# The last two chunks' second product in seven parts instead of eight, with SyncE in a planned order

## The chip, the core and the metric

The kernel runs on one core of a Trainium2 chip. Engines work side by side and meet through semaphores: TensorE (PE) multiplies, with its weight loads on a second row (PEld); VectorE (DVE), ScalarE (ACT) and GpSimd (POOL) do everything elementwise; SyncE (SP) issues nearly all DMAs. The metric is device microseconds (us) of one launch.

## The reference, cut to what matters

Inputs: q, k, v of shape 8 x 8 x 576 x 64 (batch, heads, tokens, width), g_norm of 64, and two weight matrices in 64-bit floats, w_in (512 x 2048) and w_out (2048 x 512).

```
kv  = einsum('bhsd,bhse->bhde', k, v)
x   = einsum('bhsd,bhde->bhse', q, kv)
x   = x / sqrt(mean(x*x, -1) + 1e-6) * g_norm        # to 4608 x 512
h   = x @ w_in                                       # first product, 4608 x 2048
g   = h * cos(h)
out = g @ w_out                                      # second product, 4608 x 512
```

## The kernel before

**Precision.** TensorE multiplies in a reduced 32-bit form (F32R), so each large factor is split into a high and a low half, and a product takes three matmuls: high by high, high by low, low by high. All large matmuls are 128 x 128 by 128 x 512.

**Tiling.** The 4608 tokens are nine chunks of 512. The width of 2048 is 16 strips of 128, called j, or eight pairs of strips, called m. The first three chunks (`PLAIN = 3`) are multiplied directly. Their 48 steps (`steps`, L285) each make one strip of h (`stage1_part`, L1007: 12 matmuls), then g of it (`act_part`, L1041: ACT and DVE), then add its share to four output banks (`stage2_part`, L1075: 12 matmuls). The order of steps is chunk 0 strips 0 to 3, chunk 1 strips 0 to 7, chunk 0 strips 4 to 15, chunk 1 strips 8 to 15, chunk 2. When a chunk is left unfinished its four banks are copied out and stored (`out_part`, L1108, the tensor `part`).

The other six chunks are three pairs. Their first product is Strassen's in the Winograd form: 2 x 2 blocks, seven products A11, S1, S2, A12, S4, S3, A22 instead of eight. `cross_part` (L1301) makes the seven operands from x (four of them sums), `sums_part` (L1208) the four sums of w_in for each m; the other three operands are strips as they are. `quad_part` (L1375) multiplies them for one (pair, m), 42 matmuls, adds the products together, and makes four tiles of g. The second product of these chunks is direct: a unit (`units`, L1168) is one strip j of one chunk. `split_part` (L1473) makes the high and low half of g, ACT casting and DVE or POOL subtracting, and `gather_part` (L1488) multiplies four token tiles by three matmuls: g is stationary (`lhsT`), w_out moves (`rhs`), 12 matmuls a unit, 16 units a chunk.

**Weights.** Each strip is loaded as 64-bit words (`w_loads`, L563), rebuilt and split (`w_part`, L948), and stays in SBUF for the first three chunks. Beside that, split strips are stored back to DRAM: `keep_in` (L1190, to `wq`), `keep_out` (L1201, to `wod`), and the sums to `wq` (L1239). When chunk 2 has used a strip, `freed_in` and `freed_out` (L1246, L1257) give its SBUF to the Strassen stage: the places of w_out strips 8 to 11 take weights of the first product (`t_win`), 12 to 15 those of the second (`t_wout`), strips 0 to 7 hold g and x. `load_in` and `load_out` (L1275, L1289) then stream the weights back, 512 KB a DMA.

**What sets the order.** While the program is built, `Order` (L50) plays every part as a process against guessed durations. At each point it takes the operation that can start first, ties going to the due time (`due`, L303, plus a table of offsets, `haste`, L310). Buffers are `Tokens` (taken and given back), and parts wait for `Event`s. `gates[i]` fires when step i begins on PE: `KEEP, SUMS = 16, 18` (L299) say from which step on the stores and sums may start. PE, ACT, DVE and POOL are then held to this order:

```
    pe, act, dve, pool = (Pinned(x) for x in (nc.tensor, nc.scalar, nc.vector, nc.gpsimd))
```

SyncE is not in that line. Its DMAs are issued as `nc.sync.dma_start`, and where they fall in SyncE's queue is decided by the tile framework's own scheduler. `Order` itself counts a load of several DMAs as one SyncE operation and one DMA time (`load`, L464).

**The end.** The last output tile (L1111 to L1124) is copied in two halves, one by ACT and one by DVE, each stored by its own engine's queue, in rows of 1 KB.

Of the kernel before, what the change touches and what calls it, by code (L numbers as in the profile page):

```python
# [48 lines left out]

class Order:  # L50
# [8 lines left out]
    LAT = 0.14  # L59
# [10 lines left out]
    def spawn(self, gen, t=0.0):  # L70
        proc = Proc(gen, t)
        self.live.add(proc)
        self.advance(proc, None)

    def advance(self, proc, value):
        while True:
# [18 lines left out]
            else:  # L95
# [5 lines left out]
                proc.t = max(proc.t, t)  # L101

# [32 lines left out]
    def run(self):  # L135
        while self.pending:
            best = None
            for item in self.pending:
                prio, seq, t, options, _ = item
                if len(options) == 1:  # L140
                    e, d = options[0][:2]
                else:
                    ends = [
                        max(t, self.busy.get(o[0].rstrip("*"), 0.0) + self.ahead(o[0].rstrip("*"), prio)) + o[1] + sum(o[2:])
                        for o in options
                    ]
                    e, d = options[ends.index(min(ends))][:2]
                start = self.begin(e, t)
# [20 lines left out]
def tile_kernel(  # L169
# [54 lines left out]
    pe, act, dve, pool = (Pinned(x) for x in (nc.tensor, nc.scalar, nc.vector, nc.gpsimd))  # L224

    def dve_us(f=CH, rate=1):

        return 0.15 + f / (960 * rate)

    def act_us(f=CH):  # L230
        return 0.18 + f / 1200
# [10 lines left out]
    def dve_only(f):  # L242
        return [("DVE*", 0.15 + f / 960)]
# [5 lines left out]
    def pool_us(f=CH):  # L249
        return 0.19 + f / 465  # L250
# [48 lines left out]
    KEEP, SUMS = 16, 18  # L299
# [3 lines left out]
    def due(i):  # L303
# [7 lines left out]
        ('acc', 0): 11.7, ('acc', 10): 29.9, ('acc', 11): 20.8, ('acc', 12): -117.2, ('acc', 14): 69.5,  # L311
        ('acc', 16): -23.5, ('acc', 17): 322.3, ('acc', 18): -8.2, ('acc', 19): 6.2, ('acc', 20): -28.7,
        ('acc', 21): 16.1, ('acc', 22): 20.8, ('acc', 23): -3.8, ('acc', 24): 163.5, ('acc', 25): 1.4,
        ('acc', 28): -126.9, ('acc', 29): 19.5, ('acc', 3): 177.9, ('acc', 30): -31.1, ('acc', 32): 35.7,
        ('acc', 33): -23.0, ('acc', 34): -30.3, ('acc', 37): 109.4, ('acc', 38): 19.0, ('acc', 40): -59.3,
        ('acc', 41): 142.5, ('acc', 42): 132.8, ('acc', 43): -105.5, ('acc', 44): -20.9, ('acc', 45): 3.2,
        ('acc', 46): -4.4, ('acc', 47): 497.9, ('acc', 5): 55.6, ('acc', 6): -133.7, ('acc', 7): 110.7,
        ('acc', 8): -90.2, ('acc', 9): 59.1, ('act', 0): -17.7, ('act', 1): 27.9, ('act', 10): 10.9,
        ('act', 11): -16.4, ('act', 12): 74.6, ('act', 13): 12.1, ('act', 14): -22.7, ('act', 15): -1.5,
        ('act', 16): -1.8, ('act', 17): -164.1, ('act', 18): -32.5, ('act', 19): 45.0, ('act', 2): -5.3,  # L320
        ('act', 20): 35.9, ('act', 21): -41.4, ('act', 22): 115.1, ('act', 23): -26.5, ('act', 24): -5.0,
        ('act', 25): 149.0, ('act', 26): 56.1, ('act', 27): 3.5, ('act', 28): -23.4, ('act', 29): 49.7,
        ('act', 3): -23.4, ('act', 30): -1.8, ('act', 31): -0.2, ('act', 32): -158.2, ('act', 33): -373.5,
        ('act', 34): -53.1, ('act', 35): -0.9, ('act', 36): -700.3, ('act', 37): -400.6, ('act', 38): 49.9,
        ('act', 39): -242.7, ('act', 4): -15.4, ('act', 40): 28.2, ('act', 41): 14.1, ('act', 43): -2.4,
        ('act', 44): -85.1, ('act', 45): -319.0, ('act', 46): -32.0, ('act', 47): -4.4, ('act', 5): -196.5,
        ('act', 6): -37.1, ('act', 7): -0.3, ('act', 8): 14.7, ('act', 9): -12.3, ('cross', 0, 0): -8.6,
        ('cross', 0, 1): -10.2, ('cross', 1, 0): 546.8, ('cross', 1, 1): 620.6, ('cross', 2, 0): 12.3,
# [9 lines left out]
        ('kv', 1, 3): -34.1, ('kvd', 2): -67.1, ('kvd', 3): 0.8, ('kvd', 4): 258.7, ('kvd', 5): 33.9,  # L338
        ('kvd', 6): -11.9, ('kvd', 7): 55.7, ('kvs',): 142.7, ('kvt', 4): 114.8, ('load kv', 0, 1): -242.3,
# [75 lines left out]
    def step_off(*key):  # L415
        return int(haste.get(key, 0.0) / 4)
# [1209 lines left out]
```

## Time and profile before

| | |
|---|---|
| three runs | 849.29, 849.39, 847.71 us; median 849.29 |
| the profiled execution, first to last instruction | 848.5 us |
| mean granted TensorE clock | 0.990 |
| busy: PE, DVE, ACT, POOL | 98%, 72%, 59%, 31% of the span |
| DMA, mean | 214 GB/s, 181.22 MB in 150913 packets |

The median of the runs lies 0.8 us above the profiled span. A busy PE is not PE at its peak: its matmuls overlap, so the count of matmuls by their pace tells more than the share. Every compute instruction is recorded at line 222, the helper that pins it, so groups are told apart by their tiles: `bank` is the first product (and attention), `acc` the second. Nearly all SyncE issues keep their own line.

### The profile page before, as it was taken

The page shows a single profiled execution, that of the slowest core. Times are in us where ns is not written, and L with a number is a line of the kernel's source. Part 1 is how long each engine was busy: PE and PEld are TensorE (multiplying, and loading weights), DVE is VectorE, ACT ScalarE, POOL GpSimd, SP SyncE. Part 2 cuts the span into 40 slices and gives each one's busy share as a digit, 9 for nine tenths or more (in the row PEclk, how much of TensorE's full clock was granted, in tenths as well). Part 3 has the DMA queues.
Part 4 walks back from the last instruction along what each step waited for, and adds up shares of the span by engine and source line. Part 5 has one row for each costly group of instructions (what it writes and reads, how often), then busy time and mean ns, then how long its engine had stood idle before and what let it go on. Part 6 is the DMA issues. An engine that isn't in the chain of part 4 may idle for free.

```text
span 848.5 us, 12726 instructions
## 1 busy us (share of the span) xinstructions
PE 828.0 (98%) x4376; PEld 684.0 (81%) x4376; DVE 612.9 (72%) x938; ACT 499.4 (59%) x977; POOL 266.7 (31%) x173
## 2 busy tenths in 40 slices
PE   7998999999999999999999999999989999999998
PEld 7786788888888877778888888888868888888886
DVE  4996889568497868898988887788886566454221
ACT  5886686445265655777766666776654465444321
POOL 3310003415327867561341672142445000000000
PEclk9999899999999999999999999999999999999999
DMA  9999743673744768788877767866647566763664
GB/s 314 320 342 338 289 184 114 222 176 111 221 108 123 197 171 280 248 257 260 274 246 213 211 199 201 256 207 178 194 146 255 174 177 219 221 207 115 218 211 145
DMA packets 150913, 181.22 MB, mean 214 GB/s; under 512 B 74432, under 2 KB 114112, under 8 KB 150848
## 3 DMA queue, kind: packets, MB, share of 16 engines
q1 hardware_dynamic: 150336, 179.68, 68.1%
q8 instruction: 35, 0.57, 0.3%
q10 hardware_dynamic: 512, 0.72, 0.2%
q14 instruction: 30, 0.25, 0.1%
HBM read 143.66 MB, written 36.70 MB: 213 GB/s over the span
## 4 chain that ended last, share of the span: by engine, by line
PE 89%; DMA 3%; DVE 3%; ACT 1%; SPq 1%; issue 1%; POOL 0%; ACTq 0%; DVEq 0%; POOLq 0%
PE acc L222 45%; PE bank L222 44%; DMA wo<-in_moe_w_out_dram 2%; DVE r L222 1%; DMA wi<-in_q_dram 1%; DMA sg<-in_v_dram 1%; DVE wo L222 1%; SPq L527 1%; DVE wi L222 0%; POOL rinv L222 0%; ACT slot L222 0%; DMA v_over<-in_v_dram 0%; DMA x<-slot 0%; ACT wo L222 0%; DVE glo L222 0%
## 5 line engine op out<-in xcount | busy, mean ns | idle before, releaser
L222 PE MATMUL acc<-wo,ghi 128*128 128x512 f32 x1152 | 359.2, 393 | 4.0 <-ACT slot L222 4.0
L222 PEld LDWEIGHTS acc<-wo,ghi 128*128 128x128 f32 x1152 | 216.6, 189 | 49.5 <-ACT slot L222 4.9
L222 PE MATMUL bank<-wi,wo 128*128 128x512 f32 (+2 forms) x1092 | 244.3, 379 | 4.8 <-DVE wi L222 2.6
L222 PEld LDWEIGHTS bank<-wi,wo 128*128 128x128 f32 (+2 forms) x1092 | 192.5, 185 | 46.1 <-DVE wi L222 3.0
L222 PE MATMUL acc<-wo,glo 128*128 128x512 f32 x576 | 226.3, 393 | 2.7 <-DVE glo L222 2.7
L222 POOL TENSOR_TENSOR rinv<-ms,mhalf 128x16 f32<-128x16 f32 (+1 forms) x36 | 99.1, 2754 | 152.4 <-DVE ms L222 148.6
L222 PEld LDWEIGHTS acc<-wo,glo 128*128 128x128 f32 x576 | 109.0, 189 | 27.0 <-DVE glo L222 3.9
L222 PE MATMUL bank<-xhi,wi 128*128 128x512 f32 x320 | 100.3, 395 | 0.7 <-DVE r L222 0.7
L222 DVE TENSOR_TENSOR glo<-wo,ghi 128x512 fp32r<-128x512 f32 x60 | 44.5, 743 | 54.0 <-ACT ghi L222 53.4
L222 DVE TENSOR_TENSOR wi<-bank,wi 128x512 f32<-128x512 f32 x72 | 49.4, 688 | 43.7 <-PE bank L222 35.3
L222 ACT CAST ghi<-wo 128x512 fp32r<-128x512 f32 x69 | 42.7, 620 | 64.2 <-PE acc L222 61.6
L222 PEld LDWEIGHTS bank<-xhi,wi 128*128 128x128 f32 x320 | 59.3, 189 | 13.3 <-DVE r L222 1.4
L222 ACT ACTIVATE ki<-wi 128x512 int32<-128x512 f32 x72 | 45.2, 628 | 42.2 <-DVE wi L222 36.0
L222 PE MATMUL bank<-xlo,wi 128*128 128x512 f32 x160 | 62.7, 392 | 0.0
L222 ACT COPY wi<-bank 128x512 f32<-128x512 f32 x72 | 42.0, 584 | 34.9 <-PE bank L222 31.8
L222 ACT ACTIVATE ki<-bank 128x512 int32<-128x512 f32 x72 | 42.7, 593 | 30.0 <-PE bank L222 27.0
L222 DVE TENSOR_TENSOR glo<-r,ghi 128x512 fp32r<-128x512 f32 x56 | 42.1, 753 | 22.6 <-ACT ghi L222 20.3
L222 ACT CAST ghi<-r 128x512 fp32r<-128x512 f32 x60 | 37.0, 618 | 33.2 <-PE acc L222 28.4
L222 ACT ACTIVATE wo<-wo 128x512 f32<-128x512 f32 x69 | 43.3, 629 | 19.7 <-DVE wo L222 19.5
L222 ACT ACTIVATE r<-r 128x512 f32<-128x512 f32 x60 | 37.7, 629 | 14.1 <-DVE r L222 13.2
L222 DVE TENSOR_TENSOR wo<-wo,wi 128x512 f32<-128x512 f32 x49 | 39.7, 815 | 1.3 <-ACT wo L222 1.0
L222 DVE SCALAR_TENSOR_TENSOR r<-bank,ki 128x512 f32<-128x512 f32 x51 | 34.8, 683 | 5.8 <-ACT ki L222 5.4
(169 smaller groups left out, 1091.0 us busy)
## 6 DMA issues: line engine op xcount, KB each, us to landing
wo<-wod SPq DMA_DIRECT2D x96, 512.0 KB, 3.7
wo<-wq SPq DMA_DIRECT2D x84, 512.0 KB, 4.2
out_dram<-slot SPq DMA_DIRECT2D x35, 256.0 KB, 3.4
wi<-in_moe_w_in_dram SPq DMA_DIRECT2D x16, 512.0 KB, 8.6
wo<-in_moe_w_out_dram SPq DMA_DIRECT2D x16, 512.0 KB, 7.8
wod<-wo SPq DMA_DIRECT2D x16, 512.0 KB, 5.5
wq<-wi SPq DMA_DIRECT2D x24, 256.0 KB, 3.5
m<-in_k_dram SPq DMA_DIRECT2D x24, 256.0 KB, 4.8
```

The source lines that it names most:

```text
L222: return lambda *a, **kw: tc.keep_in_program_order(f(*a, **kw))
L527: nc.sync.dma_start(out=qb[32 * e:32 * e + 32, o0 // 32:(o0 + n) // 32, :], in_=q[b, 2 * p + j, s0:s0 + n, 32 * f:32 * f + 32].rearrange(" ...
```

## The change

1. The last pair of chunks (7 and 8; `TURNED`) makes its second product by seven products too. w_out becomes the stationary factor and g the moving one, so the result comes out with w_out's columns on the partitions and tokens along the row. The strips are handled in two blocks of four m. A unit is now one of (q, m): two column sets `dt` by three matmuls, 6 matmuls, 56 units. The stationary operand takes every second of 256 columns, which are 8 bytes apart.
2. `sums_out_part` makes w_out's four sums for each m, eight passes beside those of `sums_part`, under the same token `t_sums`. `keep_out` also stores A11, A12 and S4 of w_out. All go to a new tensor `wt`, in pieces of 64 floats.
3. `parts_part` makes S1, S2, S3, S4 of g for each m. `snap_part` and `added_part` copy the banks between products and add them; the first block's sums go to DRAM and come back in the second block (`held_part`). `whole_part` and the transposes in `added_part` turn the result, which is stored in pieces of 64 floats, four DMAs for each quarter of the pair.
4. `sp` joins the pinned engines; every DMA is now its own SyncE operation in `Order`, with at most eight in flight (`t_fly`).
5. `Order`'s durations, the lower bounds of gates, `KEEP, SUMS = 11, 14`, and the whole table `haste` are new; stores and sums have offsets of their own. Tokens are now taken in a fixed order in some places (`x_begun`, `ki_taken`, `g_taken`, `t_kv`).

```diff
-    KEEP, SUMS = 16, 18
+    KEEP, SUMS = 11, 14
...
-    pe, act, dve, pool = (Pinned(x) for x in (nc.tensor, nc.scalar, nc.vector, nc.gpsimd))
+    pe, act, dve, pool, sp = (Pinned(x) for x in (nc.tensor, nc.scalar, nc.vector, nc.gpsimd, nc.sync))
...
+    t_fly = Tokens(8)
+    def dmas(pieces, prio):
+        landed = []
+        for us, issue in pieces:
+            yield "take", t_fly, prio
+            yield "run", [("SP", 0.4)], prio
+            issue()
+            landed.append(Event())
+            sched.spawn(flight(us, landed[-1]))
+        yield "wait", landed
+        return max(e.t for e in landed)
+
+    def copies(out, in_, us):
+        return us, lambda: sp.dma_start(out=out, in_=in_)
...
+    TURNED = [(NCH - PLAIN) // 2 - 1]
+    BLOCK = 4
+    turned_order = []
+    for h in range(NM // BLOCK):
+        ms = range(h * BLOCK, (h + 1) * BLOCK)
+        turned_order += [(q, m) for m in ms for q in (S1, A11)]
+        turned_order += [(q, m) for q in (S2, S4, S3, A12, A22) for m in ms]
...
     def keep_out(j, prio):
...
+        end = yield from dmas([copies(wod[j], w, 1.3)], prio)
+        if TURNED:
+            places = ((A11, 0),) if j % 2 == 0 else ((A12, 0), (S4, 1))
+            end = yield from dmas([
+                copies(turned_dram(q, m), w.rearrange("p s (a h e) -> p (s a) h e", a=NP, h=2)[:, :, half], 0.68)
+                for q, half in places], prio)
...
+    def sums_out_part(m, prio):
+        yield "wait", [w_done["wo", 2 * m], w_done["wo", 2 * m + 1]]
+        yield "take", t_sums, prio
+        pair = yield "take", t_two, prio
+        even, odd = (two(pair, [P, DM], F32, n) for n in range(2))
+        for j, t in ((2 * m, even), (2 * m + 1, odd)):
+            e, end = yield "run", adders(), prio
+            w = w_split["wo", j].bitcast(F32)
+            adder(e).tensor_tensor(out=t, in0=w[:, 0], in1=w[:, 1], op=ALU.add)
+            sched.fire(wo_read[j], end)
+        ea, eb, oa, ob = (by_half(t, i) for t in (even, odd) for i in range(2))
+        for out, a, b in ((ea, eb, ea), (eb, ob, eb), (ob, ob, ea), (oa, oa, ob)):
+            e, _ = yield "run", adders(WH), prio
+            adder(e).tensor_tensor(out=out, in0=a, in1=b, op=ALU.subtract)
+        for t, places in ((even, (S1, S3)), (odd, (A22, S2))):
+            slot = yield "take", t_slot, prio
...
+            act.copy(out=hi, in_=t)
...
+            sched.spawn(sums_store(slot, stored, prio + 20.0, [
+                copies(turned_dram(q, m)[:, n].rearrange("p (a e) -> p a e", a=NP), by_half(part, half), 0.4)
+                for half, q in enumerate(places) for n, part in enumerate((hi.bitcast(F32), t))]))
+        sched.give(t_sums, end)
...
     def freed_out(j):
-        yield "wait", [wo_used[j], wo_kept[j]]
+        after = [wo_used[j], wo_kept[j]] + ([wo_read[j]] if TURNED else [])
+        yield "wait", after
...
+    AFTER = {S2: "p1", S4: "p5", S3: "u2", A22: "c22"}
+    ACC = {A11: 0, S2: 0, S3: 0, A22: 0, S1: 2, S4: 2, A12: 2}
+    def added_part(n, h, q, dt, acc, prio):
...
+            dve.scalar_tensor_tensor(out=t, in0=acc, scalar=OUT_SCALE, in1=t, op0=ALU.mult, op1=ALU.add)
...
+            dve.transpose(out=wholes[n, i, half][:, :, :, dt], in_=t.rearrange("p (a b) -> p a b", b=32))
...
+    def whole_part(n, i, half, prio):
...
+        pieces = [
+            (out[c * CH:(c + 1) * CH, a * P + half * D:a * P + half * D + D].rearrange("(b k) f -> k b f", k=32),
+             whole[32 * a:32 * a + 32].rearrange("p b d t -> p b (d t)")) for a in range(NP)]
+        if n == (NCH - PLAIN) // 2 - 1 and i and not half:
+            for a, (to, t) in enumerate(pieces):
+                (act if a % 2 else sp).dma_start(out=to, in_=t)
+            return
...
+    def turned_unit(u, n, q, m):
...
+        for dt in range(2):
...
+            if first and q in AFTER:
+                yield "wait", [event(n, h, AFTER[q], dt)]
...
+            cols = w.rearrange("p s (n t) -> p s t n", t=2)[:, :, dt]
+            for k, (x, g) in enumerate(((0, ghi), (1, ghi), (0, glo))):
+                pe.matmul(
+                    out=accs[at + dt], lhsT=cols[:, x], rhs=g,
+                    start=(begins and k == 0), stop=(final and k == 2), skip_group_check=True)
```

More of the change, by code (lines that the diff above doesn't have):

```diff
@@ L462, in tile_kernel, with flight, load @@
     DMA_LAT = 1.6
-    def load(issue_us, us, prio, event, issue, wait=(), take=None):
+    t_fly = Tokens(8)
+    def flight(us, done):
+        _, end = yield "run", [("DMA", us)], -1e3
+        sched.give(t_fly, end + DMA_LAT)
+        sched.fire(done, end + DMA_LAT)
+    def dmas(pieces, prio):
[10 more added lines that the diff above has]
+        return us, lambda: sp.dma_start(out=out, in_=in_)
+    def load(prio, event, pieces, wait=(), take=None, first=None):
         def part():
@@ L467, in part @@
                 yield "wait", wait
+            if first:
+                yield "take", first, prio
             slot = ()
@@ L470, in part @@
                 slot = ((yield "take", take, prio),)
-            yield "run", [("SP", issue_us)], prio
-            issue(*slot)
-            _, end = yield "run", [("DMA", us)], -1e3
+            end = yield from dmas(pieces(*slot), prio)
             for ev in event:
-                sched.fire(ev, end + DMA_LAT)
+                sched.fire(ev, end)
         sched.spawn(part())
@@ L1127, in out_part @@
         if before is not None:
-            yield "run", [("SP", 0.42)], prio
-            nc.sync.dma_start(out=o, in_=before)
-            _, end = yield "run", [("DMA", 0.75)], -1e3
-            come = Event()
-            sched.fire(come, end + DMA_LAT)
-            yield "wait", [come]
+            yield from dmas([copies(o, before, 0.68)], prio)
             _, end = yield "run", [("DVE", dve_us(DM))], prio
@@ L1208, in sums_part, with sums_store @@
+    def sums_store(slot, stored, prio, pieces):
+        end = yield from dmas(pieces, prio)
+        sched.give(t_slot, end, slot)
+        for e in stored:
+            sched.fire(e, end)
     def sums_part(m, prio):
@@ L1273, in freed_x, with landing @@
                 sched.give(t_raw, max(e.t for e in (x_done[PLAIN - 1, p] for p in range(NP))), name)
+    def landing(piece, prio, events):
+        end = yield from dmas([piece], prio)
+        for ev in events:
+            sched.fire(ev, end)
     def load_in():
@@ L1327, in free @@
             yield "wait", list(after)
-            give_back(t_raw, raws[key][1], max(e.t for e in after))
+            sched.give(t_store if (TURNED and c == NCH - 2) or not (n or k) else t_raw, max(e.t for e in after), raws[key][1])
         def free_slot(slot, *after):
@@ L1483, in split_part @@
             adder(e).tensor_tensor(out=glo, in0=r, in1=ghi.bitcast(F32), op=ALU.subtract)
-            sched.give(t_store, end, held)
-            g_pairs[c, j] = ghi, glo, slot
-            sched.fire(g_split[c, j], end)
-    def gather_part():
-        for u, (c, j) in enumerate(units):
-            yield "wait", [wout_in[u], g_split[c, j]]
+            g_pairs[u] = ghi, glo, slot
+            if turned_pair:
+                sched.fire(part_split[x[1:]], end)
+            else:
+                sched.give(t_store, end, held)
@@ new lines, in tile_kernel, with event, held_part @@
+    SNAPS = {A11: "p1", S1: "p5", S2: "u2"}
+    ADDED = {S4: ("u2", 0, 1), S3: ("p5", 1, 1), A12: ("p1", 0, 0), A22: ("c21", 1, 0)}
+    ENDS_IN = {name: (i, half) for name, i, half in ADDED.values()}
+    AFTER = {S2: "p1", S4: "p5", S3: "u2", A22: "c22"}
+    ACC = {A11: 0, S2: 0, S3: 0, A22: 0, S1: 2, S4: 2, A12: 2}
+    made, held_tiles, part_sums, wholes = {}, {}, {}, {}
+    def event(*key):
+        return made.setdefault(key, Event())
+    def held_part(n, h, name, prio):
+        pair = yield "take", t_two, prio
+        tiles = [two(pair, [P, CH], F32, dt) for dt in range(2)]
+        held_tiles[n, h, name] = tiles
+        i, half = ENDS_IN[name]
+        end = sched.now()
+        if h:
+            yield "wait", [event(n, h - 1, "stored", i, half, dt) for dt in range(2)]
+            end = yield from dmas(
+                [copies(t, part_sums.pop((n, i, half, dt)), 0.68) for dt, t in enumerate(tiles)], prio)
+        sched.fire(event(n, h, "held", name), end)
+        used = [event(n, h, "used", name, dt) for dt in range(2)]
+        yield "wait", used
+        sched.give(t_two, max(x.t for x in used), pair)
@@ new lines, in snap_part @@
+    def snap_part(n, h, name, dt, acc, prio):
+        yield "wait", [event(n, h, "held", name)]
+        t = held_tiles[n, h, name][dt]
+        if h:
+            _, end = yield "run", [("DVE", dve_us())], prio
+            dve.scalar_tensor_tensor(out=t, in0=acc, scalar=OUT_SCALE, in1=t, op0=ALU.mult, op1=ALU.add)
+        else:
+            _, end = yield "run", [("ACT", act_us())], prio
+            act.activation(out=t, in_=acc, func=AF.Copy, scale=OUT_SCALE)
+        sched.fire(event(n, h, name, dt), end)
@@ new lines, in whole_part @@
+    def whole_part(n, i, half, prio):
+        c = PLAIN + 2 * n + i
+        slot = yield "take", t_cross, prio
+        whole = wholes[n, i, half] = wpool.tile([P, TB, 32, 2], F32, name=f"wi{slot}")
+        sched.fire(event(n, "whole", i, half), sched.now())
+        yield "wait", [event(n, "turned", i, half, dt) for dt in range(2)]
+        pieces = [
[5 more added lines that the diff above has]
+            return
+        end = yield from dmas([copies(to, t, 0.3) for to, t in pieces], prio)
+        sched.give(t_cross, end, slot)
@@ L1491, in gather_part @@
+    def gather_part():
+        for u, x in enumerate(units):
+            yield "wait", [wout_in[u], g_split[u]]
+            if x[0] is None:
+                yield from turned_unit(u, *x[1:])
+                continue
+            c, j = x
             for t in range(NTT):
```

690 lines of the change are left out of this document (453 added, 237 removed), and 81 rows, old and new, of the table haste.

## The prediction

> **What bounds the kernel now.** I read the page first, then the stages (busy time by window), then the chain of waits, and last the stalls.
>
> ```profile
> span 848.5 us, 12726 instructions
> PE 828.0 (98%) x4376; PEld 684.0 (81%) x4376; DVE 612.9 (72%) x938; ACT 499.4 (59%) x977; POOL 266.7 (31%) x173
> PE 89%; DMA 3%; DVE 3%; ACT 1%; SPq 1%; issue 1%; POOL 0%; ACTq 0%; DVEq 0%; POOLq 0%
> ```
>
> TensorE is the bound: 98% busy, 89% of the chain that ended last. The stages say where it is not (columns: window, its length, then each engine's busy time with its count, granted clock, DMA share, GB/s):
>
> ```profile
> 0.00:100.00 100.00, 90.29 (x697) 74.24 (x698) 75.42 (x136) 71.25 (x144) 17.88 (x21) 0.95 0.99 329
> 100.00:300.00 200.00, 199.26 (x1110) 165.74 (x1109) 156.74 (x252) 113.54 (x234) 84.75 (x55) 1.00 0.55 164
> 300.00:375.00 75.00, 71.19 (x376) 57.76 (x376) 60.81 (x80) 46.31 (x89) 49.17 (x38) 0.98 0.77 233
> 375.00:600.00 225.00, 225.00 (x1139) 186.68 (x1138) 187.64 (x287) 154.97 (x309) 83.07 (x43) 1.00 0.75 227
> 600.00:650.00 50.00, 47.31 (x201) 38.54 (x201) 41.03 (x50) 30.41 (x60) 26.66 (x15) 0.97 0.60 196
> 650.00:848.50 198.50, 194.91 (x860) 161.07 (x859) 91.25 (x135) 82.88 (x145) 5.16 (x4) 1.00 0.59 188
> ```
>
> So a matmul taken away between 375 and 848 us is worth its full time, and TensorE idles in three places: 9.7 us before 100, 3.8 in 300 to 375, 2.7 in 600 to 650. In the last two the clock also fell below 1 (0.02 of 75 us and 0.03 of 50 us, 1.5 us each): together 9.5 us lost after the start.
>
> **The front stall.** Chain of waits, then SyncE's and TensorE's timelines:
>
> ```profile
> 43.94 2.94 PE acc L222 x12
> ...
> 68.47 6.50 DMA wo<-in_moe_w_out_dram
> ...
> 75.03 7.06 DMA wo<-in_moe_w_out_dram
> ```
> ```profile
> 41.83 3.15 SPq L1196 DMA_DIRECT2D wq<-wi  x2
> ...
> 67.80 0.58 SPq L1196 DMA_DIRECT2D wq<-wi  x1
> 68.47 0.42 SPq L571 DMA_DIRECT2D wo<-in_moe_w_out_dram  x1
> 68.98 0.98 SPq L1196 DMA_DIRECT2D wq<-wi  x2
> ```
> ```profile
> 82.23 0.73 PE L222 MATMUL acc<-wo,ghi 128*128 128x512 f32 x2 [1.87 <-ACT slot L222]
> ...
> 85.36 1.22 PE L222 MATMUL acc<-wo,ghi 128*128 128x512 f32 x2 [2.17 <-ACT slot L222]
> ```
> ```profile
> 84.00:92.00 8.00, 6.64 (x16) 5.20 (x17) 6.36 (x11) 5.20 (x10) 0.00 (x0) 0.57 1.06 399
> ```
>
> TensorE waits 1.87 and 2.17 us for ACT to empty the banks; ACT had been held by two w_out loads, which took 6.50 and 7.06 us on a full DMA (share 0.99). Between the loads SyncE issues stores to `wq`. The plan gates those stores at step 16, but the first goes out at 41.83, before the first strip's second product (43.94): step 0. So the unpinned queue runs stores ahead of the plan, into the stretch that is short of bandwidth. Afterwards the clock is 0.57 for 8 us, 3.4 us lost. The stall costs 4.0 + 3.4 = 7.4 us.
>
> **The change, part by part.** *The seven products.* A stretch with nothing but the second product gives the pace:
>
> ```profile
> 779.63 65.29 PE acc L222 x288
> ```
>
> 65.29 / 288 = 0.2267 us a matmul. Before: 2 chunks x 16 strips x 12 = 384 matmuls. After: 56 units x 6 = 336. 48 x 0.2267 = **-10.9 us**, in a stage where TensorE has no slack. Each matmul's weight load must stay hidden beside it. The new one reads every second float, which no row shows; the nearest is the plain load (attention, 64 columns):
>
> ```profile
> 309.23 0.55 PEld L222 LDWEIGHTS bank<-sg,m 128*64 128x64 f32 x16
> ```
>
> 34 ns for 64 columns, an estimated 69 ns for 128, against a pitch of 227. Reading twice as slowly still hides; at four times, 276 - 227 = 49 ns show, 336 x 49 ns = +16.5 us. A gain is excluded, as hidden loads cost nothing now. I take 0, nearest the row.
>
> *Joints between products.* S2 adds into A11's bank, so its first matmul waits until A11's bank has been copied, and everything behind on TensorE waits too. Rows for the copy, the add and the transpose, and for the old tail:
>
> ```profile
> L222 ACT ACTIVATE slot<-acc 128x512 f32<-128x512 f32 x38 | 22.0, 599 | 10.7 <-PE acc L222 9.7
> L222 DVE SCALAR_TENSOR_TENSOR slot<-acc,slot 128x512 f32<-128x512 f32 x8 | 5.4, 684 | 6.3 <-DMA slot<-part 6.2
> L222 DVE STREAM_TRANSPOSE slot<-rinv 128x512 f32<-128x512 f32 x28 | 19.8, 705 | 6.1 <-POOL rinv L222 6.0
> ```
> ```profile
> 844.52 0.39 PE L222 MATMUL acc<-wo,glo 128*128 128x512 f32 x1
> ...
> 845.81 0.33 SPq L1123 DMA_DIRECT2D out_dram<-slot  x1
> ```
>
> The copy takes 0.60 us (0.68 in the second block, an add), the three matmuls of the other column set cover 0.68, and handing over costs some 0.1: 0.1 us a block, up to 0.8 if the engine is in another operation. Two blocks: 0.1 to 1.8; I take **+0.6**, a third of the way. The other waits (S4, S3, A22 on what came before) have four or more units of 1.36 us between; they are covered.
>
> *The tail.* Now 848.5 - 844.9 = 3.6 us follow the last matmul: half a copy, one issue at 845.81, and 2.7 us from that issue to the end, for 256 KB. After: add 0.68, transpose 0.70 and hand-overs of 0.1, so the first issue comes 1.5 us behind the last matmul; two DMAs on each of two queues, the second some 0.4 us later; then the 2.7 us, and more transfer, since 512 KB go in 2048 pieces of 256 bytes. Two windows bound a piece:
>
> ```profile
> DMA packets 1433, 5.23 MB, mean 209 GB/s; under 512 B 160, under 2 KB 160, under 8 KB 1432
> ...
> q1 hardware_dynamic: 1432, 5.21, 65.1%
> ```
> ```profile
> DMA packets 10385, 4.22 MB, mean 169 GB/s; under 512 B 8123, under 2 KB 9614, under 8 KB 10382
> ...
> q1 hardware_dynamic: 10382, 4.19, 66.4%
> ```
>
> The first (700 to 725 us, 4 KB packets): 0.651 x 16 x 25 us = 260 us of engine time for 5.21 MB, 50 ns a KB, so 256 bytes by size alone 12.4 ns. The second (175 to 200, mostly packets under 512 bytes): 266 us / 10382 = 25.6 ns for a packet, large ones among them, so an upper end. 2048 x 12.4 to 25.6 ns / 16 = 1.6 to 3.3 us, less 0.8 for the old 256 KB: +0.8 to +2.5. Tail 1.5 + 0.4 + 2.7 + (0.8 to 2.5) = 5.4 to 7.1, that is +1.8 to +3.5 over now; I take **+2.4**, nearer the small packets' lower end, as the 25.6 holds large ones too.
>
> *SyncE's order and the new table.* If the stores wait for their gates, the front stall goes. Bounds: 0 (another late load takes its place) to -7.4. DMA stays full there, so something will still be late: **-5**, two thirds. Pinning adds waits: an issue that is not ready holds back every DMA behind it, loads for attention and weights too. Behind 300 us late DMAs also stand on the chain:
>
> ```profile
> 304.56 2.73 DMA x<-slot
> ...
> 355.70 4.78 DMA sg<-in_v_dram
> ```
>
> Of the 9.5 us lost there and later I take **-2**, the part that is idle behind such loads; the ends are -9.5 and the slower rival's price.
>
> *Elementwise work added.* Eight passes of `sums_out_part`, gated between steps 14 and 42 or earlier; parts, adds and 24 more splits after 600. Rows of the two stretches and of POOL's sums:
>
> ```profile
> 100.00:325.00 225.00, 223.57 (x1283) 185.40 (x1282) 173.80 (x274) 126.25 (x258) 102.23 (x69) 1.00 0.56 167
> 625.00:845.00 220.00, 218.16 (x954) 180.15 (x954) 107.54 (x157) 93.73 (x167) 12.52 (x7) 0.99 0.59 190
> ```
> ```profile
> L222 POOL TENSOR_TENSOR sg<-wi 128x512 f32<-128x512 f32 x8 | 12.0, 1504 | 6.9 <-DVE wi L222 6.2 <-DVE wo L222 0.6
> L222 POOL TENSOR_TENSOR m<-m 128x256 f32<-128x256 f32 x8 | 7.7, 961 | 0.0
> ```
>
> A pass is four operations of 512 and four of 256: on POOL 4 x 1.5 + 4 x 0.96 = 9.9 us, eight passes 79 us; POOL has 225 - 102 = 123 us free. After 625: 24 splits, 32 combinations, 20 adds and 8 transposes, 84 x 0.7 = 59 us on DVE, where 112 are free, and POOL nearly idle. Nothing on the path: 0, as long as the passes end in time (below).
>
> *DMA added.* 24 stores of 1024 pieces and 64 of 512: 57344 pieces of 256 bytes, at 12.4 to 25.6 ns over 16 engines 44 to 92 us. Between 100 and 325 us the share is 0.56, so 99 us are free: hidden, though at the upper end the stretch is full. The Trainium skill, "DMA: Bandwidth & Descriptors", Specifications, speaks against this: transfers under 512 bytes fall below line rate and become read-modify-write. No row here shows a store that small; at twice the price by size, an estimate from that page, a piece costs 24.8 ns, the stretch would be full and the tail +3.4 instead of +2.4, 835.5 us in all.
>
> **Sum.** 848.5 - 10.9 + 0.6 + 2.4 - 5 - 2 = 833.6 us span; with the 0.8 us by which the runs' median lies above the span, **834.4**.
>
> **The rivals.**
> - *SyncE's order moves no stall* (it does not do what the change says, or a pinned issue waits where a late load did): only product, joints and tail count, 848.5 - 7.9 + 0.8 = 841.4. For: DMA is full before 100 us whatever the order. Against: the stores at 41.83.
> - *Every stall goes:* -7.4 and -9.5 in full, 848.5 - 7.9 - 16.9 + 0.8 = 824.5. For: 375 to 600 shows 225 us without a gap under the same kind of order. Against: more work in the same stretches.
> - *Slower: w_out's sums come too late.* `freed_out` now also waits for the sums, so no weight of the Strassen stage can be loaded into strips 8 to 15 before their passes are over. Passes share one token, now 16 in a row:
>
> ```profile
> L1239 SPq DMA_DIRECT2D wq<-slot x32: 319/422/1045, 143.5 to 381.1; - x32
> ```
>
>   Eight passes store from 143.5 to 381.1 now. The first gate moves four steps (of 24 x 0.2267 = 5.4 us) ahead, so sixteen passes have from about 120 to 300, an estimated 11.3 us each, against 9.9 of POOL's own plus casts and waits. At 13 us they end 28 us late; with some 5 us of other work in between TensorE waits 23: 841.4 + 23 = 864. From 12.1 us a pass on the gain is gone. Against: DVE can take a pass at an estimated 4.6 us, and the late half of w_in's sums isn't needed at 300.
> - *Strided weight loads show* at four times the time: 834.4 + 16.5 = 851.
>
> **Chances.** Forecast (829 to 838) 0.43; order moves no stall 0.22; every stall goes 0.18; sums too late 0.11; strided loads 0.02; the rest 0.04, as several small losses that add up to no change. A measurement here can tell about 0.2%, 1.7 us. Faster 0.83, same 0.04, slower 0.13. The range leaves out the slower rivals and the edge of the best case: 823 to 845.
>
> **What would show it.** Right: 336 `acc` matmuls with w_out first in the last pair at 0.227 us, no store to `wq` before the late w_out loads, no gap at 80 to 86 us, 5 to 7 us behind the last matmul. Wrong: weight loads above 227 ns in the last pair; gaps on TensorE around 300 to 350 that end on DMA of weights or on POOL; SyncE waiting on a store while loads stand behind it; a new gap at 640 to 840 that ends on the split or the parts.

## The result, and the profile after

The changed kernel takes 862.28 us (median; 859.97 to 863.89), the kernel before 849.34 beside it: a ratio of 1.0147, 95% interval 1.0123 to 1.0172 (the two medians alone give 1.0152). It is slower by 1.5%, where 834.4 us were forecast.

The page of the profiled execution after, the fastest of four (span, busy time of each engine, and the engines of the chain that ended last):

```profile
span 858.2 us, 12977 instructions
PE 824.1 (96%) x4328; PEld 671.8 (78%) x4328; DVE 673.8 (79%) x1029; ACT 521.3 (61%) x1025; POOL 317.1 (37%) x220
PE 70%; DMA 14%; DVE 7%; ACT 3%; SPq 3%; issue 1%; ACTq 0%; DVEq 0%
```

TensorE does 48 matmuls less and is still the bound, but 14% of the chain is now DMA (3% before) and 7% DVE. The stages (busy time by window, columns as in the prediction):

```profile
0.00:100.00 100.00, 91.12 (x707) 74.92 (x708) 83.00 (x147) 78.66 (x161) 18.74 (x21) 0.97 1.03 333
100.00:300.00 200.00, 195.71 (x1079) 159.35 (x1077) 153.03 (x233) 106.83 (x218) 111.60 (x83) 1.00 0.72 199
300.00:375.00 75.00, 68.61 (x361) 55.03 (x362) 58.47 (x79) 46.92 (x93) 50.68 (x40) 0.98 0.80 232
375.00:600.00 225.00, 217.40 (x1091) 176.04 (x1090) 203.00 (x317) 161.22 (x328) 91.50 (x49) 1.00 0.83 241
600.00:650.00 50.00, 50.00 (x221) 41.03 (x221) 40.36 (x53) 28.74 (x55) 22.98 (x14) 1.00 0.66 206
650.00:858.20 208.20, 201.26 (x876) 165.46 (x874) 135.91 (x205) 98.92 (x175) 21.60 (x14) 1.00 0.66 207
```

TensorE's idle time, window less busy time, before and after:

| us | before | after | difference |
|---|---|---|---|
| 0 to 100 | 9.7 | 8.9 | -0.8 |
| 100 to 300 | 0.7 | 4.3 | +3.6 |
| 300 to 375 | 3.8 | 6.4 | +2.6 |
| 375 to 600 | 0 | 7.6 | +7.6 |
| 600 to 650 | 2.7 | 0 | -2.7 |
| 650 to the end | 3.6 | 6.9 | +3.3 |

The sum is +13.6 us of idle time; busy time falls by only 3.9 (828.0 to 824.1), and +9.7 is the difference of the spans. Most of the idle time gained is small stalls from 100 to 600 us, in stages that the new product never enters (its first weights are loaded at 730 us). Before, 375 to 600 had none. TensorE's longest waits:

```profile
PE bank L239 <- DMA wo<-wq: 8.1, 6, 3.0
PE bank L239 <- DVE r L239: 3.2, 5, 1.2
PE bank L239 <- DVE xlo L239: 2.3, 2, 2.1
```

The first are loads of Strassen weights for the first product. The chain of waits has them one after another. Ahead of the first stand copies of output tiles by ACT and SyncE issues:

```profile
336.48 0.91 ACT slot L239 x2
...
339.25 0.38 SPq L239
...
339.72 4.30 DMA wo<-wq
344.16 4.58 PE bank L239 x12
348.76 3.50 DMA wo<-wq
...
373.35 5.09 DMA wo<-wq
...
406.35 5.17 DMA wo<-wq
...
452.44 5.25 DMA wo<-wq
```

SyncE's timeline names these issues. They are stores of the output tiles that ACT has just copied, and the load stands behind them in the held queue; TensorE then waits 2.96 us for it, the longest wait of this kind:

```profile
337.94 1.69 SPq L239 DMA_DIRECT2D out_dram<-slot  x3
339.72 1.16 SPq L239 DMA_DIRECT2D wo<-wq  x2
```

Where the new stores lie (the tile `wt`: count, duration of an issue, first and last start), and how full the DMA is from 375 to 450 us:

```profile
L239 SPq DMA_DIRECT2D wt<-slot x32: 359/504/1392, 142.6 to 443.7; - x32
...
L239 SPq DMA_DIRECT2D wt<-wo x24: 359/472/1803, 55.5 to 419.4; - x24
```
```profile
DMA packets 29593, 21.26 MB, mean 284 GB/s; under 512 B 24032, under 2 KB 26080, under 8 KB 29586
...
q1 hardware_dynamic: 29586, 21.18, 98.8%
...
wo<-wq SPq DMA_DIRECT2D x15, 512.0 KB, 5.5
...
wt<-slot SPq DMA_DIRECT2D x12, 128.0 KB, 5.2
...
wt<-m SPq DMA_DIRECT2D x6, 128.0 KB, 4.7
wt<-sg SPq DMA_DIRECT2D x6, 128.0 KB, 4.3
...
wt<-wo SPq DMA_DIRECT2D x1, 256.0 KB, 3.9
```

The stores start at 55 us, before the stretch that was counted free, and end at 445, well behind it. By their pieces (512 of each 128 KB store, 1024 of each 256 KB store), 33792 of the 57344 lie between 100 and 300 us, 8192 before, 2048 in 300 to 375 and 13312 in 375 to 450. In 375 to 450 us the DMA is full.

### The profile page after: what moved, and what is told of

The parts are those of the page before. It is cut to its first block, busy times and chain, and to the rows that moved or that the text cites. A ratio compares the mean times of both kernels' runs of the same rounds, so it can differ in the third digit from the quotient of the medians.

```text
span 858.2 us, 12977 instructions
## 1 busy us (share of the span) xinstructions
PE 824.1 (96%) x4328; PEld 671.8 (78%) x4328; DVE 673.8 (79%) x1029; ACT 521.3 (61%) x1025; POOL 317.1 (37%) x220
## 4 chain that ended last, share of the span: by engine, by line
PE 70%; DMA 14%; DVE 7%; ACT 3%; SPq 3%; issue 1%; ACTq 0%; DVEq 0%
PE acc L239 38%; PE bank L239 32%; DMA wo<-wq 4%; SPq L239 3%; DMA wo<-in_k_dram 2%; DMA wo<-in_moe_w_out_dram 1%; DVE wi L239 1%; DMA wi<-in_moe_w_in_dram 1%; DMA qb<-in_q_dram 1%; DMA x<-slot 1%; DVE sg L239 1%; DMA wo<-in_v_dram 1%; DVE wo L239 1%; DMA slot<-part 1%; DVE qT L239 1%
## 5 line engine op out<-in xcount | busy, mean ns | idle before, releaser
L239 PE MATMUL acc<-wo,ghi 128*128 128x512 f32 x896 | 278.1, 391 | 2.1 <-DVE slot L239 1.9
L239 PE MATMUL bank<-wi,wo 128*128 128x512 f32 (+2 forms) x1092 | 247.1, 382 | 12.7 <-DMA wo<-wq 8.1
L239 PEld LDWEIGHTS acc<-wo,ghi 128*128 128x128 f32 x896 | 166.5, 188 | 37.7 <-DVE slot L239 3.2
L239 PE MATMUL acc<-wo,glo 128*128 128x512 f32 x448 | 175.0, 391 | 0.3 <-DVE glo L239 0.3
L239 PEld LDWEIGHTS acc<-wo,glo 128*128 128x128 f32 x448 | 84.1, 188 | 19.3 <-DVE glo L239 1.6
L239 ACT ACTIVATE ki<-bank 128x512 int32<-128x512 f32 x72 | 42.7, 593 | 30.5 <-PE bank L239 27.7
L239 DVE TENSOR_TENSOR glo<-wo,ghi 128x512 fp32r<-128x512 f32 x48 | 34.6, 720 | 27.1 <-ACT ghi L239 25.2
L239 ACT CAST ghi<-wo 128x512 fp32r<-128x512 f32 x53 | 32.8, 619 | 23.5 <-PE acc L239 22.0
L239 DVE TENSOR_TENSOR glo<-r,ghi 128x512 fp32r<-128x512 f32 x53 | 38.7, 736 | 9.9 <-ACT ghi L239 7.5
L239 DVE SCALAR_TENSOR_TENSOR r<-bank,ki 128x512 f32<-128x512 f32 x50 | 34.3, 686 | 12.6 <-ACT ki L239 12.2
L239 ACT ACTIVATE wo<-wo 128x512 f32<-128x512 f32 x54 | 34.0, 629 | 13.9 <-DVE wo L239 13.7
L239 PE MATMUL acc<-wi,wo 128*128 128x512 f32 x162 | 38.4, 394 | 0.0
```

The lines of the kernel that those rows point to most:

```text
L239: return lambda *a, **kw: tc.keep_in_program_order(f(*a, **kw))
```

## The experiments

Each ratio is to the kernel before, run on the same chip. A profile shows one run of several, and not always one near the median; where it matters, the text says which.

### The stores of `wt`: absent, tiny, in larger pieces

Three kernels keep the planner's prices, and so the order of every queue. `no_wt` leaves the 88 stores out:

```diff
-                copies(turned_dram(q, m), w.rearrange("p s (a h e) -> p (s a) h e", a=NP, h=2)[:, :, half], 0.68)
+                (0.68, lambda: None)
...
-                copies(turned_dram(q, m)[:, n].rearrange("p (a e) -> p a e", a=NP), by_half(part, half), 0.4)
+                (0.4, lambda: None)
...
-                src, n = wt[first // 2], 2
+                src, n = wod[first // 2 % NJ].rearrange("p s (x y) -> p s x y", x=2), 2
```

> The changed kernel without the 88 stores of w_out's operands (its weights for the last pair's second product are read from w_out itself instead, so the last two chunks' result is another). Order and elementwise work stay. If the added DMAs (their traffic and their places in SyncE's queue) cost the time: 847 to 853 us, idle time of TensorE in 100 to 450 us down from some 18 us to under 8. If the order, or the elementwise work, costs it: 858 or more.

`tiny_wt` issues all 88, each of 8 columns:

```diff
+                copies(turned_dram(q, m)[:, 0, 0:8], w[:, 0, 0:8], 0.68)
...
+                copies(turned_dram(q, m)[:, n, 0:8], part[:, 0:8], 0.4)
```

> The changed kernel in its own order, all 88 stores of w_out's halves and sums issued at their places but of 8 columns each (32-byte pieces), the loads of them taken from the stored w_out tiles instead. Left out: the rest of those stores. Theory (bytes: 57344 pieces of 256 B fill the DMA engines): as without the stores, 851 to 855 us. Rival (SyncE's issues and its waits in a held order cost, not the bytes): as the changed kernel, 859 to 863.

`contiguous` stores a half as two runs of 256 columns (1 KB pieces) and takes the output's columns accordingly:

```diff
-    w.rearrange("p s (a h e) -> p (s a) h e", a=NP, h=2)[:, :, half]
+    w[:, :, half * WH:(half + 1) * WH]
```

> The changed kernel with w_out's halves taken as two runs of 256 columns, so that the pieces of wt are 1 KB instead of 256 bytes; the order of all engines is as it was. 57344 small packets become 14336. If the bandwidth of small pieces matters: 854 to 859 us, DMA share between 175 and 200 us under 0.97 (1.03 now). If it does not: 860 to 864.

| | us | ratio, 95% |
|---|---|---|
| changed kernel | 862.28 | 1.0147 (1.0123 to 1.0172) |
| 1 KB pieces (`contiguous`) | 858.45 | 1.0093 (1.0063 to 1.0123) |
| tiny stores (`tiny_wt`) | 855.11 | 1.0057 (1.0038 to 1.0076) |
| no stores (`no_wt`) | 853.06 | 1.0031 (1.0009 to 1.0054) |

The DMA from 375 to 450 us without the stores, and the windows of that kernel:

```profile
DMA packets 16832, 17.77 MB, mean 237 GB/s; under 512 B 11685, under 2 KB 13241, under 8 KB 16825
...
q1 hardware_dynamic: 16825, 17.69, 78.9%
...
wo<-wq SPq DMA_DIRECT2D x16, 512.0 KB, 4.4
```
```profile
100.00:300.00 200.00, 198.47 (x1102) 163.73 (x1102) 157.37 (x242) 109.24 (x226) 116.45 (x86) 1.00 0.54 159
300.00:375.00 75.00, 67.25 (x353) 53.16 (x352) 57.93 (x76) 46.30 (x88) 49.13 (x39) 0.98 0.81 242
375.00:600.00 225.00, 220.14 (x1106) 179.36 (x1106) 204.14 (x320) 162.46 (x333) 88.11 (x47) 1.00 0.75 225
```

The stores cost 0.0116 of 849.3, 10 us. Three quarters of it goes when only the bytes go (1.0147 to 1.0057, 7.6 us), so it is DMA time; what the 88 issues cost on SyncE (1.0057 against 1.0031) isn't told from nothing. The same bytes in 1 KB pieces give back 4.6 us, though the share in 175 to 200 us only falls from 1.03 to 0.99. In 375 to 450 us the share falls from 98.8 to 78.9% without the 13312 pieces: 0.199 x 16 x 75 us / 13312 = 17.9 ns for a piece of 256 bytes (12761 packets less in all, as the other traffic is not quite the same). A load of Strassen weights there lands in 4.4 us instead of 5.5 (medians). That fits stores that slow the loads; how much comes from buffers that the stores hold for longer isn't told apart.

Between the two profiled executions, 7.5 us apart, TensorE's idle time falls by 3.5 us and its busy time by 4.0 (824.1 to 820.1), with the same 4328 matmuls; so the price of the stores doesn't show in the idle times alone, and why the matmuls are busy for longer isn't resolved. The idle time that went lies in 100 to 300 us (2.8) and 375 to 600 (2.7). But 300 to 375 us keeps its own (7.8 us against 6.4), and 4.9 remain behind it: 12.6 us in 100 to 450, where under 8 was expected. The rest has another cause.

### The sums' elementwise work

`slim` cuts the four subtractions of half tiles and the two of low halves in each pass of `sums_out_part` to 8 columns; `no_wt_slim` does that and leaves the stores out as well.

```diff
-            adder(e).tensor_tensor(out=out, in0=a, in1=b, op=ALU.subtract)
+            adder(e).tensor_tensor(out=out[:, 0, 0:8], in0=a[:, 0, 0:8], in1=b[:, 0, 0:8], op=ALU.subtract)
...
-            adder(e).tensor_tensor(out=t, in0=t, in1=hi.bitcast(F32), op=ALU.subtract)
+            adder(e).tensor_tensor(out=t[:, 0:8], in0=t[:, 0:8], in1=hi[:, 0:8].bitcast(F32), op=ALU.subtract)
```

> The changed kernel with six of the eight operations on DVE or POOL in each pass of w_out's sums cut to 8 columns a part (four subtractions and the two low halves), so the sums of w_out are not the right ones; the order and all DMAs stay. If the added elementwise work in 100 to 450 us holds TensorE up: 852 to 858 us. If the added DMAs are what counts and the operations only fill free time: 860 to 864.

> The changed kernel in its own order without the 88 stores, and with the six subtractions of half tiles or low halves of each pass over w_out cut to 8 columns. Left out: those stores and the rest of those subtractions. Theory (without the stores what is left over the kernel before is order, 3 us of tail and 2 us of strided loads): 851 to 854, as without the stores alone (853.06). Rival (the work of the sums hides behind the stores and shows once they are gone): 842 to 848.

`slim`: 860.38 us, 1.0135 (1.0090 to 1.0180). `no_wt_slim`: 849.72 us, 1.0003 (0.9979 to 1.0028). The pairs differ by 0.0012 and 0.0028, 1.0 and 2.4 us, with intervals that overlap: not resolved. `slim` lies where the DMAs alone were to count; `no_wt_slim` lies between the two ranges, 851 to 854 and 842 to 848, and decides for neither. Its stages from 300 us, in the fastest of ten runs:

```profile
300.00:375.00 75.00, 69.10 (x371) 54.89 (x369) 59.39 (x82) 49.89 (x95) 47.05 (x41) 1.00 0.81 247
...
375.00:600.00 225.00, 222.52 (x1115) 181.09 (x1116) 202.36 (x323) 162.92 (x334) 84.44 (x48) 1.00 0.75 226
```

With the stores and most of that work gone, 300 to 600 us of this run still holds 5.9 + 2.5 = 8.4 us of idle time against 3.8 before.

### The stationary operand read densely

```diff
-            cols = w.rearrange("p s (n t) -> p s t n", t=2)[:, :, dt]
+            cols = w.rearrange("p s (t n) -> p s t n", t=2)[:, :, dt]
```

> The changed kernel with the stationary operand of the last pair's second product read as 128 neighbouring floats instead of every second one; its output columns then come out in another order. If the strided weight load slows the matmuls: the last 120 acc matmuls take 27.2 us (0.2267 each) instead of 28.25, and the whole run 2 to 3 us less. If the slower pace has another cause (writes of DVE and ACT beside it): 28 us or more, and no change of the time.

858.50 us, 1.0106 (1.0080 to 1.0132). Unbroken stretches of the new product, and weight loads from 790 to 852 us, first of the changed kernel, then of this one:

```profile
797.83 25.20 PE acc L239 x108
...
823.16 28.25 PE acc L239 x120
```
```profile
L239 PEld LDWEIGHTS acc<-wi,wo 128*128 128x128 f32 x162 | 31.3, 193 | 6.5
```
```profile
799.61 24.48 PE acc L239 x108
...
824.24 27.49 PE acc L239 x120
```
```profile
L239 PEld LDWEIGHTS acc<-wi,wo 128*128 128x128 f32 x162 | 30.4, 188 | 6.3
```

53.45 us for 228 matmuls against 51.97: 6.5 ns a matmul, 336 x 6.5 ns = 2.2 us. A load that is 5 ns longer shows, though it is shorter than the pitch. The difference of the ratios, 3.5 us, agrees within their intervals.

### SyncE's order, apart from the product

`unpinned` is the changed kernel with SyncE in the framework's order (shown); `before_pinned` the kernel before with SyncE held (the reverse, with its `nc.sync.dma_start` as `sp.dma_start`).

```diff
-    pe, act, dve, pool, sp = (Pinned(x) for x in (nc.tensor, nc.scalar, nc.vector, nc.gpsimd, nc.sync))
+    pe, act, dve, pool = (Pinned(x) for x in (nc.tensor, nc.scalar, nc.vector, nc.gpsimd))
+    sp = nc.sync
```

> The changed kernel with SyncE's DMAs issued unpinned again, everything else as changed. If the held order of SyncE's queue is what costs (loads of the first product's weights stand behind stores that are not ready), the loss against the kernel before goes largely: 845 to 853 us, and TensorE's idle time on wo<-wq (8.1 us now) falls under 3. If the added work and DMA traffic cost it, the time stays at 858 to 866. If the front gains from the held order, the idle time before 100 us grows from 8.9 us.

> The kernel before with SyncE pinned to program order, nothing else. If holding the queue costs by itself: 855 us or more, with new idle time of TensorE behind DMA. If holding it is harmless or helps (my prediction had -5 us at the front): 840 to 849, and the stores to wq leave the first 60 us.

`unpinned`: 883.99 us, 1.0400 (1.0361 to 1.0439), above both ranges that were expected. `before_pinned`: 850.36 us, 0.9997 (0.9978 to 1.0016), between its two. The changed plan needs the held queue (883.99 - 862.28 = 21.7 us); for the plan before it is worth nothing. The first 100 us of each, and what `before_pinned` waits for; its profile is of the slowest of ten runs, 854.96 us:

```profile
0.00:100.00 100.00, 70.88 (x602) 56.94 (x602) 58.89 (x106) 56.44 (x121) 20.28 (x21) 0.86 1.01 320
```
```profile
0.00:100.00 100.00, 91.64 (x723) 75.76 (x724) 80.84 (x144) 75.44 (x151) 17.77 (x21) 1.00 0.74 242
...
375.00:600.00 225.00, 219.18 (x1102) 181.25 (x1101) 182.78 (x279) 149.81 (x300) 79.34 (x42) 0.98 0.72 222
```
```profile
PE bank L222 <- DMA wo<-wq: 6.3, 2, 5.8
```

Held, the front does what the prediction said: the clock is 1.00 instead of 0.95, the DMA share 0.74 instead of 0.99, and the stores of split w_in to `wq` start at 114 us instead of 42. Idle time before 100 us falls only from 9.7 to 8.4, and in this run a weight load is 5.8 us late in 375 to 600, which had no gap before. That the stores put off make it late isn't shown: the last of them is issued at 258.8 us. Ahead of the load SyncE issues eight loads of q for 7.2 us, then stores of the sums, which had the same place before:

```profile
373.80 7.21 SPq L222 DMA_DIRECT2D qb<-in_q_dram  x8
...
386.01 0.42 SPq L222 DMA_DIRECT2D wo<-wq  x1
```

Whether the faster runs have this wait isn't on record.

### How much hangs on the table of offsets

`seven_gx` is the changed kernel without the offsets called "gate x"; `eight_gx` the same with the second product in eight parts (`TURNED = []`).

```diff
+    haste = {a: b for a, b in haste.items() if a[0] != 'gate x'}
...
-    TURNED = [(NCH - PLAIN) // 2 - 1]
+    TURNED = []
```

> A control for the next run: the changed kernel with the offsets 'gate x' (when attention parts of later chunks may begin) left out of the table, as the plan without the seven products does not come to an end with them. Seven products stay. A table that was searched for with them should be the better one: 860 to 875 us.

> The same as seven_gx, but TURNED is empty: the last pair's second product is direct again (eight parts), with no sums of w_out, no wt, no turned output; SyncE held, the new table and the new durations stay. If the seven products' side work (stores, sums, joints, tail) costs more than the 48 matmuls save: faster than seven_gx by 5 to 20 us, and near or under the kernel before (850). If the new table and the held order cost it: within 5 us of seven_gx or slower, by up to 11 us.

931.10 us (1.0970, 1.0931 to 1.1009) and 878.84 (1.0357, 1.0315 to 1.0398). Both expectations missed by far: dropping 27 offsets costs 69 us, and the seven parts are 52 behind. A table fits one plan only, so two plans can be compared only if each has a table made for it. The next runs do that.

### The planner's prices

`Order` is a model with prices, and its own last time can be read when the kernel is built: 828.2 us before, 819.8 after. So the change promised 8.4 us; the chip lies 21.1 above the plan before and 42.5 above it after (medians). One sort of price is too low: a store of 1024 pieces takes 1024 x 17.9 ns / 16 = 1.15 us (mean of the trace's packets of 256 bytes) and is priced 0.68. And the change lowered the elementwise prices: 512 columns cost 0.065 + 512/960 = 0.598 us on DVE (0.683 before), 0.527 on ACT (0.607 before). The old ones are near the length of one record in the changed kernel (mean ns behind the busy time):

```profile
L239 DVE TENSOR_TENSOR wi<-bank,wi 128x512 f32<-128x512 f32 x72 | 49.0, 686 | 29.9 <-PE bank L239 25.0 <-ACT ki L239 4.3
L239 ACT CAST ghi<-r 128x512 fp32r<-128x512 f32 x56 | 34.6, 621 | 20.9 <-PE acc L239 11.8 <-DVE r L239 8.6 <-DVE ms L239 0.4
```

But the records of one engine overlap when it has no wait between them. In the kernel before, two operations of 512 columns in a row take 1.15 us on ACT and 1.29 on DVE:

```profile
778.60 1.15 ACT L222 ACTIVATE wo<-wo 128x512 f32<-128x512 f32 x2
...
779.41 1.29 DVE L222 TENSOR_TENSOR wo<-wo,wi 128x512 f32<-128x512 f32 x2
```

With some 0.63 and 0.69 us for one record, the second starts 0.52 and 0.60 us after the first. The lowered prices are near this pace and the old ones near the length, so the groups above don't show the lowered ones to be too low.

Five kernels with a table found anew, by small changes kept where they bring the plan's last time down, and with prices changed. `seven_repriced`:

```diff
-                copies(turned_dram(q, m), w.rearrange("p s (a h e) -> p (s a) h e", a=NP, h=2)[:, :, half], 0.68)
+                copies(turned_dram(q, m), w.rearrange("p s (a h e) -> p (s a) h e", a=NP, h=2)[:, :, half], 1.15)
...
-                copies(turned_dram(q, m)[:, n].rearrange("p (a e) -> p a e", a=NP), by_half(part, half), 0.4)
+                copies(turned_dram(q, m)[:, n].rearrange("p (a e) -> p a e", a=NP), by_half(part, half), 0.58)
...
-            _, end = yield "run", [("PE", 0.68)], due_unit(u) + dt * 0.01 + put_off("unit", u)
+            _, end = yield "run", [("PE", 0.7)], due_unit(u) + dt * 0.01 + put_off("unit", u)
```

`contig_repriced` is `contiguous` with 0.74 and 0.37 there. `eight_repriced` has neither stores nor strided matmuls, only its table and `TURNED = []`. `seven_elem` and `eight_elem` are the seven and eight parts with the elementwise prices of the kernel before:

```diff
-    LAT = 0.13
+    LAT = 0.14
...
-        return 0.065 + f / (960 * rate)
+        return 0.15 + f / (960 * rate)
...
-        return 0.1 + f / 1200
+        return 0.18 + f / 1200
...
-        return 0.16 + f / 465
+        return 0.19 + f / 465
```

> The changed kernel with three prices of its planner corrected to what the trace shows (store of a half tile of w_out 0.68 to 1.15 us, of a sum's half 0.4 to 0.58 us, three strided matmuls 0.68 to 0.70 us) and a table of offsets found anew for them; the instructions are the same, only their order differs. The changed kernel's planner ends at 819.8 and the chip at 858.2 (38.4 more), the kernel before plans 828.2 and takes 848.5 (20.3 more); this one plans 825.9. Theory (the order was laid out on prices that are too low, and its stalls are the difference): the excess falls back to about 20, a span near 846 to 849 and a time of 847 to 850. Rival (the stalls belong to the seven parts whatever the order): excess 34 to 40, a time of 860 to 866.

> The same code with the second product in eight parts for all chunks (no half tiles of w_out stored, no sums of w_out), SyncE held, a table found anew in the same way; plans 826.0. Theory (the seven parts save 10.9 us of matmul and give it back in the order that the stores force): a time of 844 to 850, level with the seven parts under true prices within 4 us. Rival (the seven parts are worth their matmuls once the order is right): 5 us or more above the seven parts under true prices.

> Seven parts, w_out's halves stored as two runs of 256 columns (1 KB pieces, priced 0.74 and 0.37 us), the output's columns taken accordingly, table found anew; plans 824.5. Theory of prices: a time of 844 to 848, below both kernels by a little. Rival (stalls belong to the seven parts): 855 to 860 as the run with 1 KB pieces and the old table (858.45).

> Seven parts, planned with the elementwise prices of the kernel before (DVE 0.15 + f/960 in place of 0.065 + f/960, ACT 0.18 in place of 0.1, POOL 0.19 in place of 0.16, latency 0.14) and the true prices of stores and strided matmuls, table found anew; the instructions are those of the changed kernel. Plans 856.5. Theory (a plan on true prices keeps its promise, about 20 us under the chip as for the kernel before): 874 to 880. Rival (the plan on low prices is the better order on the chip, and true prices only show the load): 857 to 868.

> Eight parts, planned with the same elementwise prices, table found anew; plans 833.3, 23.2 below the seven parts. Theory: 852 to 856, the seven parts 20 us or more behind. Rival (the difference of the two is set by the chip's own stalls, not by the plan): the seven parts 5 to 12 behind, as under the low prices (857.99 against 848.81).

| | plan | chip | above the plan | ratio, 95% |
|---|---|---|---|---|
| `seven_repriced` | 825.9 | 857.99 | 32.1 | 1.0092 (1.0071 to 1.0114) |
| `eight_repriced` | 826.0 | 848.81 | 22.8 | 0.9991 (0.9974 to 1.0008) |
| `contig_repriced` | 824.5 | 864.51 | 40.0 | 1.0165 (1.0139 to 1.0192) |
| `seven_elem` | 856.5 | 876.47 | 20.0 | 1.0315 (1.0271 to 1.0358) |
| `eight_elem` | 833.3 | 848.79 | 15.5 | 0.9977 (0.9961 to 0.9993) |

Corrected store prices with their table bring back 4.7 us (1.0147 to 1.0092), not the 14 that the theory asked for; 857.99 lies between its range and the rival's. They fail altogether for 1 KB pieces, where both expectations missed. With equal plans and tables of the same making, seven parts are 9.2 us behind eight, where 4 at most were expected. Between the two, the stage where the first product of the pairs begins differs most (300 to 375 us, seven parts first, in the fastest of six runs; the eight parts' profile is of the slowest of twelve, 853.53 us):

```profile
300.00:375.00 75.00, 68.29 (x364) 55.05 (x363) 62.31 (x82) 46.84 (x95) 53.62 (x41) 0.98 0.77 231
```
```profile
300.00:375.00 75.00, 75.00 (x335) 62.02 (x334) 59.60 (x84) 47.79 (x92) 21.34 (x15) 1.00 0.62 186
```

There the eight parts keep TensorE full with a DMA share of 0.62; the seven idle for 6.7 us. The work in that window isn't the same (335 matmuls against 364, POOL busy for 21 us against 54), so this shows that the orders differ, not why. Under the higher elementwise prices the plan for seven parts falls 23 us behind that for eight, the chip follows (27.7; the eight parts themselves are faster than the 852 to 856 that were expected), and the distance from plan to chip is 15 to 20 us again. A plan with higher prices promises less in any case, so the smaller distance doesn't show that they are right. The orders found with them are no better: 848.79 against 848.81 us for eight parts, and `seven_elem` is 18.5 us slower than `seven_repriced`. So the elementwise prices move the promise; that they cost the changed kernel its time isn't shown.

`eight_elem` is the only kernel here that lies below the kernel before by more than its interval, and only just, by 0.23% (0.9977, 0.9961 to 0.9993): the new planning with SyncE held, without the seven parts.

## Why the prediction was wrong, point by point

- **The product, -10.9.** Right in its mechanism: 336 matmuls instead of 384. The strided weight loads were put at 0 and cost 2.2 us (`dense_w`). The argument "shorter than the pitch, so hidden" failed; the row used (64 columns, 34 ns) did not stand for loads of 128 columns, whose own mean of 189 ns the page had, not the estimated 69.
- **Joints, +0.6.** TensorE waits for nothing from 640 us to its last matmul, so the joints cost 0.
- **The tail, +2.4.** The last matmul ends near 851.4 us, 6.8 before the end, against 3.6: +3.2, within the bounds.

```profile
851.00 0.40 PE L239 MATMUL acc<-glo,wo 128*128 128x512 f32 x1
```

- **Added DMA, 0: the step that the runs show to have failed.** The size was right: at 17.9 ns a piece 57344 pieces take 64 us, inside the 44 to 92. The Trainium skill, "DMA: Bandwidth & Descriptors", Specifications, puts transfers under 512 bytes below line rate, and the runs agree, 17.9 ns against 12.4 by size (12.8 when the window is worked out again); the doubling that I estimated from its read-modify-write (24.8) isn't seen. What failed is the place: the 99 us that were free lie between 100 and 325 us, while stores ran from 55 to 445. On average that stretch had room for all of them: with 33792 pieces its share in 100 to 300 us is 0.72, so 56 us are still free, and the other 23552 take 26. But 13312 went into 375 to 450, where the share is 0.79 without them, and 8192 before 100. In place of 0 the stores cost 10 us (`no_wt` against the changed kernel).
- **SyncE's order, -5 and -2: the largest miss, shown in part.** The step "if the stores wait for their gates" failed, as the new plan doesn't make them wait: in the changed kernel 16 of the 24 stores of split w_in to `wq` start before 100 us (15 before), and 8 of `wt` with them. First and last issue, before and after:

```profile
L1196 SPq DMA_DIRECT2D wq<-wi x24: 359/371/1737, 41.8 to 141.9; - x24
```
```profile
L239 SPq DMA_DIRECT2D wq<-wi x24: 359/498/2877, 45.5 to 199.7; - x24
```

  So the sign "no store to `wq` before the late w_out loads" is missing and the DMA share before 100 us rose from 0.99 to 1.03. The stall at 80 to 86 us went even so (75 to 100 us: TensorE busy for 25.00 us instead of 20.96), but 0 to 25 us lost 2.3; the front gave 0.8 in idle time. And where the stores are put off (`before_pinned`), the time doesn't fall: the rival "the order moves no stall" (0.22) was right about the net effect, 0.9997, though not in its mechanism, since the stall did move. Behind 300 us stalls were added, not taken away. The longest is of a kind that the prediction had listed under "wrong": a load that stands behind stores in SyncE's queue (339.72 us).
- **Elementwise work, 0.** 1.0 and 2.4 us for six operations of each pass, not resolved, so 0 is neither refuted nor confirmed. That the change lowered the planner's elementwise prices by some 12% wasn't weighed at all; whether it matters isn't shown either.
- **"Sums come too late"** (0.11) named the right place, loads of `wo` behind 300 us, and a loss; its sign, gaps that end on loads of weights, came. The passes do run late: the last stores of w_out's sums are issued at 443 to 445 us, not by 300. That they hold back the places for weights isn't shown; what is shown goes with the stores' bytes.

**The ledger.** -10.9 product, +2.2 strided loads, +3.2 tail, +10 stores: +4.5. Measured +12.5 (1.0147). Of the 8 us left, 6 are the idle time from 300 to 600 us that stays without stores (12.6 us in `no_wt` against 3.8), less the 2.7 that ended at 600 to 650. Beside the forecast, product, joints and tail came out at -5.5 instead of -7.9, the stores at 10 instead of 0, and all the rest, where the forecast had SyncE's order at -7, at +8. Seven parts have 10.0 and 12.6 us idle there under two new tables, stores included (`seven_repriced`, `seven_elem`), eight parts 5.3 and 2.3 (`eight_repriced`, `eight_elem`), each in one profiled run. The cause of these 8 us isn't settled; the queue at 339.72 us is one stall of them, and `no_wt` has it as well (three output stores at 332.77, the load at 334.69, a wait of 2.06 us). Whether an order for seven parts exists without it, stays open: the release of w_out's places by the sums (`wo_read`) and SyncE's head of line were not separated from it.

## What to carry to other kernels

An added transfer is hidden only if it lies where the bandwidth is free: ask for the window of its first and last issue, not for the sum. A kernel whose order comes from a planner inherits its prices; compare each with the trace first, the pace of operations in a row as well as the length of one, and judge a change by two plans each with its own table. Here a gain of 1.3% in matmuls didn't pay for 14.7 MB of new stores; a kernel that keeps them all inside the free stretch was not run.

## What the runs showed of the hardware

A weight load of 193 instead of 188 ns, under a pitch of 228, lengthened the pitch by 6.5 ns. Pieces of 256 bytes took 17.9 ns (mean), those of 1 KB 49 to 51, so a byte costs 1.4 times as much in small pieces. Operations of 512 columns in a row started 0.60 us apart on DVE and 0.52 on ACT, though one record lasted some 0.69 and 0.63.
